# Re-opening four PSUM banks as single-bank tiles once attention has left them

## The chip, the cores and the metric

One core of a Trainium2 chip runs the whole program in one launch. The metric is the device time of the execution in microseconds (us). All runs told of here count as fast (within 1.5% of the fastest run of their kernel); where their clocks differ, in experiment 9, the text says so. The time of a run is some 1.8 us longer than the span of its profile. The granted TensorE clock of a profiled run is given where it matters. PE is the matmul engine (TensorE), PEld its weight loads, DVE is VectorE, ACT is ScalarE.

## The reference

Block-causal attention (8 batches, 8 heads, 576 positions, 64 per head) followed by a token mixer and a channel mixer over the model's 512 columns. The part that matters here is the channel mixer of the last batches, which runs after the last attention scores:

```python
u = x + (np.maximum(x.transpose(0, 2, 1) @ w_tok1, 0.0) @ w_tok2).transpose(0, 2, 1)
h2 = np.maximum(u @ w_ch1, 0.0) @ w_ch2     # w_ch1: 512 x 1536, w_ch2: 1536 x 512
out = u + h2
```

The kernel computes these products in seven block products instead of eight, which makes many evictions from PSUM: a block product is copied out (`keep`), added to another (`join`), or clipped at zero. The sums run on DVE, the copies and clips on DVE or ACT.

## The kernel before

The kernel holds eight banks of PSUM. Attention needs pairs of banks, because one exponential reads two banks at once (95 of them read 128x1024 from `sc` in the trace before, 1.02 us each by the median); everything else needs one. So the kernel has four single banks (`mm`) and two tiles of two banks (`sc`). When the last attention scores have been read, the four banks of `sc` go to a pool of slots named `late`, and matmuls take a slot from `mm` or from `late`.

```python
sc = ring(2, [128, 2, 512], FP32, "sc", psum)     # two tiles of two banks
mm = ring(4, [128, 512], FP32, "mm", psum)        # four tiles of one bank
...
P.pool("mm", mm)
P.pool("late", [])                                # empty until attention ends
BANK = ("mm", "late")
...
def bank_of(note):
    n = note["slot"]
    return mm[n] if note["pool"] == "mm" else sc[n // 2][:, n % 2]
...
# the exponentials of the last score set hand their two banks over as two slots each
freed = [[{"pool": "late", "slot": 2 * f + i} for i in range(2)] if last else None for f in range(2)]
...
# a block product takes a slot; its last reader gives it back
op = P.add("PE", mm_cost(512, 2), emit, deps + [last.get(to)], ..., take=[(BANK, bank)] if first else ())
...
with tc.manual_schedule():
    for op in P.search(1000):      # the order on each engine comes from a search at build time
        op.emit(op)
```

Two things do not see each other here. The search counts slots, so for it the two halves of an `sc` tile are independent. The layer that inserts the semaphores guards a tile: in the built program, a matmul into one half waits for the reader of the other half, and a reader of one half waits for matmuls into the other. The trace before shows both: the matmul at 205.82 us stood idle for 0.28 us by the profile's count, until the DVE add that read the other half had ended at 205.77 us, and the DVE copy at 261.57 us stood idle for 1.05 us while twelve matmuls went into the other half.

The softmax here doesn't subtract the row's maximum and nothing guards it: scores larger than these inputs give would overflow.

## Time and profile before

| | before |
|---|---|
| time, median of 3 (296.56 to 296.77) | 296.73 us |
| span of the profiled run | 294.8 us |
| PE busy in 196 to 232, 232 to 256, 256 to 272 us | 35.13, 23.95, 15.00 us |
| PE waits from 196 us on | four, all on `sc` banks, 1.7 us counted |

The way to read these: PE is busy almost all the time (285.8 us, 97% of the span), so only an idle gap of PE can be won. What such a gap really costs is worked out in the prediction below, which also shows the lines.

### The profile page before, as it was taken

How to read it: one execution, taken by the hardware profiler on the slowest of the kernel's cores; microseconds unless marked ns; L12 is line 12 of the kernel's file. 1: busy time of each engine (PE TensorE's matmuls, PEld its weight loads, DVE VectorE, ACT ScalarE, POOL GpSimd, SP SyncE). 2: the span in 40 equal slices, each digit the busy share in tenths (PEclk: the TensorE clock that was granted, in tenths of full speed). 3: DMA queues.
4: the chain of work that ended last, by engine and by line, in shares of the span. 5: the costliest groups of instructions: out<-in, count | busy, mean ns of one | idle time of the engine just before them, and what ended most of it. 6: DMA issues, size and time to landing. Idle time of an engine off the chain costs nothing.

```text
span 294.8 us, 7653 instructions
## 1 busy us (share of the span) xinstructions
PE 285.8 (97%) x3232; PEld 180.4 (61%) x3252; DVE 236.4 (80%) x512; ACT 166.9 (57%) x236; POOL 62.1 (21%) x96
## 2 busy tenths in 40 slices
PE   8999999999999999999999999999999999989994
PEld 4566456564557755545765567774446885556884
DVE  5566668988859979959988978678998968959993
ACT  5897874667776564786566685524476004847000
POOL 8776353810520260260050000000000000000000
PEclk9999999999999999999999999999999999999999
DMA  8999999993793399992359030041000811130054
GB/s 212 187 191 210 206 186 183 226 205 83 122 124 57 49 174 220 146 124 44 72 38 190 2 71 2 2 162 36 3 0 20 142 73 71 36 142 2 1 176 148
DMA packets 64403, 31.99 MB, mean 109 GB/s; under 512 B 53104, under 2 KB 55024, under 8 KB 64368
## 3 DMA queue, kind: packets, MB, share of 16 engines
q0 software_dynamic: 44320, 17.34, 50.1%
q1 hardware_dynamic: 19760, 13.57, 17.1%
q10 hardware_dynamic: 288, 0.59, 0.6%
q8 instruction: 25, 0.41, 0.5%
q14 instruction: 10, 0.08, 0.1%
HBM read 35.85 MB, written 9.44 MB: 154 GB/s over the span
## 4 chain that ended last, share of the span: by engine, by line
PE 87%; ACT 6%; DVE 4%; DMA 1%; issue 1%; ACTq 0%; DVEq 0%
PE mm L1221 17%; PE mm L992 15%; PE sc L548 9%; PE mm L595 9%; PE mm L1312 7%; PE mm L781 6%; PE sc L1097 5%; PE mm L1097 5%; PE sc L1221 4%; ACT e_sb L567 4%; PE mm L874 4%; PE mm L1019 3%; DVE turned L433 2%; DMA gT<-in_k_dram 1%; DVE gT L1125 1%
## 5 line engine op out<-in xcount | busy, mean ns | idle before, releaser
L567 ACT ACTIVATE e_sb<-sc 128x1024 bf16<-128x1024 f32 x95 | 92.5, 1030 | 32.9 <-PE sc L548 32.3
L992 PE MATMUL mm<-uT,wc_sb 128*128 128x512 bf16 x192 | 46.1, 382 | 0.0
L462 POOL DMA_DIRECT2D vals<-in_v_dram x45 | 37.0, 837 | 27.0 <-PE mm L595 22.4
L433 DVE STREAM_TRANSPOSE turned<-raws 128x288 int32<-128x288 int32 x64 | 40.2, 707 | 2.4 <-ACT raws L393 1.5
L548 PE MATMUL sc<-turned 32*128 32x64 bf16 (+4 forms) x744 | 35.4, 281 | 1.0 <-ACT e_sb L567 0.4
L595 PEld LDWEIGHTS <-e_sb 128*128 128x128 bf16 x896 | 31.3, 97 | 6.7 <-issue 3.2
L992 PEld LDWEIGHTS <-wc_sb 128*128 128x128 bf16 x192 | 20.0, 115 | 20.7 <-issue 5.7
L595 PE MATMUL mm<-vals,e_sb 128*128 128x65 bf16 x868 | 32.5, 193 | 0.1
L623 DVE TENSOR_TENSOR x_sb<-mm,rinv 128x320 bf16<-128x320 f32 x62 | 29.1, 485 | 1.3
L769 DVE TENSOR_SCALAR gT<-mm 128x512 bf16<-128x512 f32 x27 | 18.6, 688 | 10.9 <-PE mm L992 10.8
L1221 PEld LDWEIGHTS <-sums 128*128 128x128 bf16 x252 | 24.1, 98 | 4.5 <-issue 1.2
L1221 PEld LDWEIGHTS <-gT 128*128 128x128 bf16 x240 | 22.9, 98 | 4.5 <-issue 1.3
L548 PEld LDWEIGHTS <-turned 32*128 32x128 bf16 x752 | 12.8, 93 | 19.3 <-issue 16.7
L393 ACT COPY e_sb<-mm 128x512 f32<-128x512 f32 x14 | 8.2, 591 | 27.6 <-PE mm L1097 26.1
L767 ACT ACTIVATE gT<-mm 128x512 bf16<-128x512 f32 x24 | 14.3, 597 | 10.9 <-PE mm L992 10.8
L573 DVE MEMSET e_sb<- 64x128 uint32 (+1 forms) x72 | 10.6, 153 | 9.7 <-ACT e_sb L567 5.7
L781 PE MATMUL mm<-x_sb,w_sb 128*128 128x512 bf16 (+1 forms) x97 | 17.6, 313 | 0.3
L413 POOL DMA_DIRECT2D raws<-in_k_dram x15 | 8.2, 549 | 40.0 <-DVE turned L433 31.4
L889 DVE TENSOR_TENSOR u_sb<-mm,x_sb 128x512 bf16<-128x512 f32 x24 | 15.4, 684 | 1.4 <-PE sc L548 0.7
L1244 DVE TENSOR_TENSOR o_sb<-mm,u_sb 128x512 f32<-128x512 f32 x20 | 13.7, 687 | 3.4 <-PE mm L1221 2.6
L1097 PEld LDWEIGHTS <-raws 128*128 128x128 bf16 x96 | 9.2, 98 | 10.9 <-issue 1.5
L1221 PE MATMUL mm<-wd_sb,sums 128*128 128x256 bf16 x132 | 15.7, 273 | 0.0
(146 smaller groups left out, 458.0 us busy)
## 6 DMA issues: line engine op xcount, KB each, us to landing
out_dram<-o_sb SPq DMA_DIRECT2D x14, 512.0 KB, 3.2
raws<-in_k_dram POOLq DMA_DIRECT2D x15, 288.0 KB, 6.0
raws<-in_q_dram POOLq DMA_DIRECT2D x15, 288.0 KB, 6.8
vals<-in_v_dram POOLq DMA_DIRECT2D x28, 128.0 KB, 6.4
wc_sb<-in_moe_w_ch_dram POOLq DMA_DIRECT2D x8, 192.0 KB, 6.6
wc_sb<-in_moe_w_ch_dram POOLq DMA_DIRECT2D x3, 512.0 KB, 10.5
out_dram<-o_sb SPq DMA_DIRECT2D x10, 128.0 KB, 2.3
vals<-in_v_dram POOLq DMA_DIRECT2D x15, 64.0 KB, 5.6
```

The source lines that it names most:

```text
L433: nc.vector.transpose(dst[:, 0:S, :] .rearrange("p s e -> p (s e)") .bitcast(I32) .rearrange("p (a k) -> p k a", k=NB)[:, k0:k1], raw2.bit ...
L462: nc.gpsimd.dma_start(out=dst, in_=src)
L548: nc.tensor.matmul(out=home(n)[:, c0 : c0 + w], lhsT=kT[i][r, j0 : j0 + 128, par], rhs=qT[i][r, i0 : i0 + w, par], start=(par == 0), stop= ...
L567: nc.scalar.activation(dst, sc[SC.index(note["pool"])][:, :, 0:n], EXP, scale=scale)
L595: nc.tensor.matmul(out=u[:, I, 0:65], lhsT=w, rhs=vt[:, J, head, 0:65], start=(J == 0), stop=(J == I),)
L623: nc.vector.tensor_tensor(out=xt[:, :, 64 * head : 64 * head + 64], in0=u[:, :, 0:64], in1=ri.to_broadcast([128, 5, 64]), op=MULT,)
L769: nc.vector.tensor_scalar_max(dst, src, 0.0)
L781: nc.tensor.matmul(out=bank_of(bank)[:, w * n : w * n + w], lhsT=wt[:, tt : tt + 255 : 2], rhs=xt[:, c, cols], start=(c == 0), stop=(c == 4),)
L992: nc.tensor.matmul(out=bank_of(bank), lhsT=wc1_sb[:, m, channels(cc)], rhs=uT[b % 2][:, :, m, :], start=(m == 0), stop=(m == NDM - 1),)
L1097: nc.tensor.matmul(out=bank_of(bank), lhsT=x(m), rhs=y[:, :, m, :], start=first and m == 0, stop=m == 1, skip_group_check=not first,)
L1221: nc.tensor.matmul(out=bank_of(bank)[:, 256 * i : 256 * i + 256], lhsT=x[:, kk, 128 * i : 128 * i + 128], rhs=y[:, kk], start=first and i ...
L1312: nc.tensor.matmul(out=ps, lhsT=gt[:, cc, c0 : c0 + 128], rhs=wc2_sb[:, cc, cols], start=(cc == 0 and not turned), stop=(cc == NDC - 1),)
```

## The change

The intent is that the matmuls after attention see four single banks. The pool with the pairs is closed and a new pool is opened over the same memory at the moment when the first `late` slot is used. So that the pool of the pairs can be closed while that of `mm` stays open, `mm` is now allocated before `sc`.

```diff
-    sc = ring(2, [128, 2, 512], FP32, "sc", psum)
     mm = ring(4, [128, 512], FP32, "mm", psum)
+    held_banks = [tc.tile_pool(name="pairs", bufs=1, space=bass.MemoryType.PSUM)]
+    sc = ring(2, [128, 2, 512], FP32, "sc", held_banks[0].__enter__())
+    late = []
...
     def bank_of(note):
-        n = note["slot"]
-        return mm[n] if note["pool"] == "mm" else sc[n // 2][:, n % 2]
+        if note["pool"] == "mm":
+            return mm[note["slot"]]
+        if not late:
+            held_banks[0].__exit__(None, None, None)
+            held_banks[0] = tc.tile_pool(name="singles", bufs=1, space=bass.MemoryType.PSUM)
+            late.extend(ring(4, [128, 512], FP32, "late", held_banks[0].__enter__()))
+        return late[note["slot"]]
...
+    held_banks[0].__exit__(None, None, None)
```

## The prediction

> **What bounds the kernel now.** I read the page first, then busy time by stretch, then the waits of the matmul engine, then its timeline around each wait. The page's first section already says who is the bound:
>
> ```profile
> PE 285.8 (97%) x3232; PEld 180.4 (61%) x3252; DVE 236.4 (80%) x512; ACT 166.9 (57%) x236; POOL 62.1 (21%) x96
> ```
>
> The clock row of the page is 9 in all 40 slices, so no throttling is to be won back. The diff touches only tiles that are used after the last attention scores, and the timeline has the first matmul that writes one of those re-used banks (the weighted sum of values, L595 into `sc`) at 196.25 us. So I cut the span there; columns are stretch, its length, then busy us of PE, PEld, DVE, ACT, POOL:
>
> ```profile
> 0.00:196.00 196.00, 192.73 (x2532) 117.86 (x2549) 153.98 (x372) 131.41 (x178) 62.06 (x96) 1.00 0.91 129
> 196.00:232.00 36.00, 35.13 (x253) 19.95 (x254) 32.77 (x58) 16.35 (x29) 0.00 (x0) 1.00 0.18 39
> 232.00:256.00 24.00, 23.95 (x166) 16.40 (x165) 20.51 (x32) 7.69 (x13) 0.00 (x0) 1.00 0.30 80
> 256.00:272.00 16.00, 15.00 (x117) 9.63 (x117) 11.65 (x20) 10.97 (x17) 0.00 (x0) 1.00 0.18 67
> ```
>
> The change cannot act on the first 196 us. In the rest PE is idle for only 0.87, 0.05 and 1.00 us in the three stretches shown. Whatever is won is won out of those few gaps. The waits of PE from 196 us on name them all:
>
> ```profile
> PE sc L1097 <- DVE o_sb L1244: 0.9, 1, 0.9
> PE sc L1097 <- ACT e_sb L393: 0.5, 2, 0.3
> PE sc L874 <- DVE gT L1125: 0.3, 1, 0.3
> ```
>
> All four waits are for an `sc` bank, none for an `mm` bank: the single-bank tiles never hold PE up for long here, the paired ones do. The timeline shows what stood before each (start, length, engine, line, count, idle time):
>
> ```profile
> 204.94 0.59 PE L874 MATMUL mm<-aT,w_sb 128*128 128x512 bf16 x2
> 205.82 1.02 PE L874 MATMUL sc<-aT,w_sb 128*128 128x512 bf16 x4 [0.28 <-DVE gT L1125]
> ...
> 208.63 0.59 PE L1097 MATMUL mm<-e_sb,raws 128*128 128x512 bf16 x2
> 209.51 0.59 PE L1097 MATMUL sc<-uT,wc_sb 128*128 128x512 bf16 x2 [0.29 <-ACT e_sb L393]
> ...
> 219.59 0.59 PE L1097 MATMUL sc<-uT,wc_sb 128*128 128x512 bf16 x2
> 220.38 0.59 PE L1097 MATMUL sc<-e_sb,wc_sb 128*128 128x512 bf16 x2 [0.19 <-ACT e_sb L393]
> ...
> 261.37 0.59 PE L1097 MATMUL mm<-e_sb,wc_sb 128*128 128x512 bf16 x2
> 262.91 0.59 PE L1097 MATMUL sc<-uT,raws 128*128 128x512 bf16 x2 [0.95 <-DVE o_sb L1244]
> ```
>
> Pairs of matmuls that follow without a wait start 0.43 us apart (209.51 to 209.94 in the same timeline), so 0.216 us per matmul of 512 columns, though each row is longer. The idle time in brackets is counted from the modelled end; the time lost is counted from the start that the cadence would have given. That is more: 205.82 - (204.94 + 0.43) = **0.45**; 209.51 - 209.06 = **0.45**; 220.38 - 220.02 = **0.36**; 262.91 - 261.80 = **1.11** us.
>
> [...] here rows of 0.376 us start 0.216 us apart, which is why I reckon with starts.
>
> **The change part by part.** Its code is bookkeeping at build time. The schedule is chosen over slots, not tiles, and the comparison of the two built programs confirms that every engine has the same instructions in the same order (6,505 on PE, 513 on DVE, 239 on ACT); neither a copy nor a memset is added. What differs is the semaphore waits. I resolved each wait of both programs to the instruction that satisfies it. About 17 matmuls, 7 ScalarE and 13 VectorE instructions differ, of which these matter:
>
> 1. *Re-opening the pool.* The first matmul into a new tile gains a wait for the last score matmul, on its own engine and past. The last ScalarE exponential ended at 193.88 us, before 196.25. Cost 0.
> 2. *Matmul at 205.82* (second bank of pair 1) waited for a VectorE add that read the first bank (205.07 to 205.77). Gone; nothing else holds it. Gain 0.45.
> 3. *Matmul at 209.51* waited for the ScalarE copy at 208.88 of the other bank. What remains is its own bank's reader, a VectorE add done at 207.14. Gain 0.45.
> 4. *Matmul at 220.38* waited for the ScalarE copy at 219.74 of the other bank. What remains is an add at 219.02 to 219.70, which in the present timing alone would give nearly everything, and which itself moves up (see 6). Gain 0.36.
> 5. *Two small ones.* The matmul at 222.22 lost 0.12 us to an add on its neighbour: gone. The one at 219.16 loses 0.15 us to a true wait on an `mm` bank, whose add moves up: probably gone.
> 6. *VectorE reads that waited for matmuls into the neighbour.* The adds at 207.44 (0.30 us idle) and at 216.62 (0.57 idle) waited for a write to the other half. VectorE is busy 32.77 of 36 us there, so these count: without them VectorE keeps up with the earlier PE.
> 7. *Matmul at 262.91.* It waited for the add at 262.18, which stood behind a copy:
>
> ```profile
> 261.57 0.69 DVE L395 COPY e_sb<-sc 128x512 f32<-128x512 f32 x1 [1.05 <-PE sc L1221]
> 262.18 0.68 DVE L1244 TENSOR_TENSOR o_sb<-sc,u_sb 128x512 f32<-128x512 f32 x1
> ```
>
> The copy sat idle for 1.05 us for twelve L1221 matmuls into the other bank, although its own bank was complete at about 260.2. In the changed kernel it starts when VectorE is free (the add before it ends at 260.52), ends near 261.2, and the matmul needs only that copy: it starts at its natural 261.80. Gain 1.11.
>
> Sum: 0.45 + 0.45 + 0.36 + 0.12 + 0.15 + 1.11 = **2.64 us**. Nothing of it lies beside other work, because PE has no other idle time between 196 us and its last matmul.
>
> Will the earlier PE run into true waits? I took the slack between each matmul and the end of its other releasers, and moved both up. After 209 us PE is 0.9 us early and VectorE only about 0.45, then 0.57. Three matmuls become tight: those at 211.24, 214.26 and 216.42 come out at -0.02 to +0.07 us of slack. From 216.62 on VectorE is 1.2 us early and PE 0.9, then about 1.5 from 222 us. From 226 to 260 us slacks are 0.34 us or more and VectorE mostly follows PE. After 262.91 everything is 2.64 us early; the last stage has slacks of 0.4 or more that shift with PE. I allow 0.25 us for the tight places, so a gain of 2.4: 296.73 - 2.4 = **294.3 us**.
>
> **Rivals.** (a) *VectorE becomes the bound between 205 and 222 us and returns the early part.* For: it is 91% busy there, with almost no idle time from 210 to 216. Against: two of its own waits go too. It would leave the 1.11 us and perhaps half of the 1.5: about 295.0. (b) *The 262.91 wait is only moved*: the copy or the sums arrive as late for another reason. For: ScalarE's clip at 260.55 runs 1.06 us beside it. Against: it isn't a releaser of this matmul. It would cost most of 1.11: about 295.5. (c) *Nothing at all*, if waits through a semaphore's running count still cover the neighbour[...]. I counted in these; it would stay at 296.7. (d) *Slower*: a second drain of banks at the re-opening stalls PE. The resolved waits speak against it: no engine gains a late one.
>
> **Range and chances.** The measured runs differ by 0.2 us. A full gain with all tight places free gives 294.0, rivals (a) and (b) together 296. I take 293.7 to 295.4. A gain of over 2% would need 5.9 us, and PE has only 1.9 us of counted idle time in the three stretches: 1%. Slower by 2% needs a fault that neither program shows: 1%.
>
> **What would show it.** PE idle waits on re-used banks after 196 us should all but vanish (from 1.7 us in the list of waits to under 0.4). The copy of L395 before the old 262.91 place should no longer wait for L1221. The span up to 196 us should be the same to 0.1 us. New waits on `mm` banks, released by VectorE, near 210 to 216 us would be rival (a). The prediction is wrong if PE's idle time goes but the end doesn't move by it, or if earlier matmuls bring a slower cadence than 0.216 us.

## The result, and the profile after

The changed kernel took 294.19 us (median of 6, 294.04 to 294.74); the kernel before took 296.69 us in its 6 runs. The ratio is 0.9915 (95% interval 0.9902 to 0.9928). Ratios here are the mean time of one kernel's fast runs over that of the other's fast runs of the same rounds, so they are not quite the ratio of the medians. The prediction was 294.3 us.

The busy time by stretch of the changed kernel, with the columns of the prediction's table:

```profile
0.00:196.00 196.00, 194.18 (x2548) 117.83 (x2549) 153.53 (x372) 131.50 (x178) 61.97 (x96) 1.00 0.91 129
196.00:232.00 36.00, 36.00 (x269) 21.27 (x268) 33.89 (x60) 16.28 (x29) 0.00 (x0) 1.00 0.22 45
232.00:256.00 24.00, 24.00 (x166) 16.32 (x164) 20.48 (x33) 9.09 (x14) 0.00 (x0) 1.00 0.25 71
256.00:272.00 16.00, 16.00 (x128) 10.49 (x126) 12.90 (x21) 9.89 (x16) 0.00 (x0) 1.00 0.18 67
```

PE has no idle time at all from 196 us on, and the list of its waits from there is empty. (The first line counts 1.45 us more PE time than before, though the work is the same: the trace before has 20 fewer matmul records, 16 of them in this stretch.) The timeline of PE around two of the old waits, start, length, engine, line, count:

```profile
205.05 0.59 PE L881 MATMUL mm<-aT,w_sb 128*128 128x512 bf16 x2
205.48 1.03 PE L881 MATMUL late<-aT,w_sb 128*128 128x512 bf16 x4
...
259.97 0.59 PE L1104 MATMUL mm<-e_sb,wc_sb 128*128 128x512 bf16 x2
260.40 0.59 PE L1104 MATMUL late<-uT,raws 128*128 128x512 bf16 x2
```

Both pairs now start 0.43 us apart, which is two matmuls at the cadence: before, 0.88 and 1.54 us. On DVE, the copy that held the second of them no longer waits for L1228 (L1221 of the kernel before), while the add after it does, for its own bank:

```profile
259.22 0.69 DVE L402 COPY e_sb<-late 128x512 f32<-128x512 f32 x1
260.17 0.69 DVE L1251 TENSOR_TENSOR o_sb<-late,u_sb 128x512 f32<-128x512 f32 x1 [0.26 <-PE late L1228]
```

Because both programs have the same instructions in the same order, each matmul of one trace can be laid on its twin in the other. The difference of their starts changes at six places. In the rest it is flat, apart from places where a matmul's record is missing from the trace before:

| matmul, by its start before | predicted step, us | measured step, us |
|---|---|---|
| 205.82 | 0.45 | 0.45 |
| 209.51 | 0.45 | 0.45 |
| 219.16 | 0.15 | 0.15 |
| 220.38 | 0.36 | 0.35 |
| 222.22 | 0.12 | 0.12 |
| 262.91 | 1.11 | 1.11 |
| sum | 2.64 | 2.62 |

The profiled run of the changed kernel had started its first scores 0.13 us later and was still 0.11 us behind at 205 us, so PE ended 2.51 us earlier, 288.49 against 291.00 us. From there to the end of the span it took 3.92 us in place of 3.77, so that the span is 2.37 us shorter (292.40 against 294.77); why the end took longer was not looked into. The medians differ by 2.50.

### The profile page after: what moved, and what is told of

It reads as the page before. It is cut to its first block, busy times and chain, and to the rows that moved or that the text cites. A ratio compares the mean times of both kernels' runs of the same rounds, so it can differ in the third digit from the quotient of the medians.

```text
span 292.4 us, 7674 instructions
## 1 busy us (share of the span) xinstructions
PE 286.7 (98%) x3252; PEld 180.4 (62%) x3252; DVE 235.7 (81%) x512; ACT 166.8 (57%) x236; POOL 62.0 (21%) x96
## 4 chain that ended last, share of the span: by engine, by line
PE 93%; ACT 4%; DVE 1%; issue 0%
PE mm L1228 18%; PE mm L999 15%; PE sc L555 9%; PE mm L602 9%; PE mm L1319 7%; PE mm L1104 6%; PE late L1104 6%; PE mm L788 6%; PE late L1228 4%; PE mm L881 4%; ACT e_sb L574 4%; PE mm L1026 3%; PE mm L372 2%; DVE turned L440 1%; PE mm L912 1%; PE mm L379 0%
## 5 line engine op out<-in xcount | busy, mean ns | idle before, releaser
L1228 PEld LDWEIGHTS <-sums 128*128 128x128 bf16 x252 | 24.1, 98 | 4.4 <-issue 1.2
L1228 PEld LDWEIGHTS <-gT 128*128 128x128 bf16 x240 | 22.9, 98 | 4.5 <-issue 1.3
L1251 DVE TENSOR_TENSOR o_sb<-mm,u_sb 128x512 f32<-128x512 f32 x20 | 13.7, 686 | 3.4 <-PE mm L1228 2.6
L1228 PE MATMUL mm<-wd_sb,sums 128*128 128x256 bf16 x132 | 15.7, 273 | 0.0
L1251 DVE TENSOR_TENSOR o_sb<-mm,o_sb 128x512 f32<-128x512 f32 (+1 forms) x19 | 12.0, 631 | 4.4 <-PE mm L1228 4.2
```

The source lines that it names most:

```text
L1228: nc.tensor.matmul(out=bank_of(bank)[:, 256 * i : 256 * i + 256], lhsT=x[:, kk, 128 * i : 128 * i + 128], rhs=y[:, kk], start=first and i ...
L1251: nc.vector.tensor_tensor(out=dst, in0=src, in1=other, op=ADD)
```

## The experiments

The theory is that the width of the guarded tile sets the price: matmuls and readers of different banks wait for one another when one tile covers both. A false wait is a wait for a reader or a matmul of another bank, which only the shared tile imposes. The rivals are that the re-opening or the new order of the pools did it, that each false wait is worth just what its own matmul lost (the local account, against the chain theory, by which a wait can pass its delay on through DVE and ACT), and that the last stage was short of banks. Twelve runs were made, two of them repeats; all gave correct results, and that narrower guards are safe is shown by no more than this. Each ratio is to the kernel before. The edits below are to the changed kernel unless said otherwise.

**1. Re-opened as two pairs.**

```diff
-            late.extend(ring(4, [128, 512], FP32, "late", held_banks[0].__enter__()))
-        return late[note["slot"]]
+            late.extend(ring(2, [128, 2, 512], FP32, "late", held_banks[0].__enter__()))
+        return late[note["slot"] // 2][:, note["slot"] % 2]
```

> As the changed kernel, with the banks re-opened as two tiles of two banks, slots 0+1 and 2+3 as before. My theory (the width of the tile that is guarded is all that counts): every false wait is back, at the old places (matmuls near 205.8, 209.5, 220.4 and 262.9 us), 296.7 us, within 0.3 of the kernel before. Rival (the closing and re-opening of the pool, or the other order of the PSUM pools, is what gained): 294.2 us.

Measured: 296.86 us, ratio to before 1.000 (0.9992 to 1.0008). The four waits were back at 205.83, 209.49, 220.34 and 262.88 us. So neither the closing and re-opening nor the order of the pools gains or costs anything that can be seen (the interval is 0.24 us either way): the gain is in the width of the tile.

**2 and 3. Only one of the pairs split.** In the first, slots 0 and 1 are single and 2 and 3 are one tile; in the second, the other way round.

```diff
-            late.extend(ring(4, [128, 512], FP32, "late", held_banks[0].__enter__()))
+            again = held_banks[0].__enter__()
+            singles = ring(2, [128, 512], FP32, "late", again)
+            pair = ring(1, [128, 2, 512], FP32, "latepair", again)[0]
+            late.extend(singles + [pair[:, 0], pair[:, 1]])    # second kernel: pair first, then singles
```

> Only slots 0 and 1 become single banks; 2 and 3 stay one tile. Local account (each matmul's own false wait is worth what it lost): 0.12 + 1.11 = 1.2 us gained, 295.45 us. Theory of chains: VectorE's add near 216.6 us, which waited for a neighbour in pair 0, also starts some 0.6 us earlier; the ScalarE copy behind the wait near 220.4 us (a pair 2+3 wait that stays in this kernel) then ends in time, and so does the true wait near 219.2 us. Gained 0.15 + 0.36 + 0.12 + 1.11 = 1.75 us, so 294.95 us, with the false waits at 205.8 and 209.5 still there (0.45 us each) and none near 220.

> Only slots 2 and 3 become single banks; 0 and 1 stay one tile. Local account: 0.45 + 0.45 + 0.36 = 1.26 us gained, 295.4 us. Theory of chains: the two early gains of 0.45 stay, but VectorE still loses time to false waits in pair 0, so what is won near 220.4 us is lost again at the wait near 222.2 us, which grows from 0.12 to about 0.46 us; gained 0.9 us, 295.8 us. The 1.1 us wait near 262.9 us (then near 262.0) is still there in either case.

Measured: with slots 0 and 1 split, 295.38 us, ratio 0.9948 (0.9935 to 0.9961), which lay between the two accounts; with slots 2 and 3 split, 295.90 us, ratio 0.9969 (0.9956 to 0.9982), that is 0.9 us gained (0.5 to 1.3), where the chain theory had 0.9 and the local account 1.26. This interval takes in both, so the traces have to tell. Their PE waits after 196 us follow, all of them (the edits move the lines: L1097 of the kernel before is L1107 and L1106 here). First with slots 0 and 1 split:

```profile
206.45 0.59 PE L884 MATMUL latepair<-aT,w_sb 128*128 128x512 bf16 x2 [0.28 <-DVE gT L1135]
210.10 0.59 PE L1107 MATMUL latepair<-uT,wc_sb 128*128 128x512 bf16 x2 [0.24 <-ACT e_sb L403]
```

Then those with slots 2 and 3 split:

```profile
221.47 0.59 PE L1106 MATMUL latepair<-e_sb,raws 128*128 128x512 bf16 x2 [0.31 <-DVE gT L1134]
262.15 0.59 PE L1106 MATMUL latepair<-uT,raws 128*128 128x512 bf16 x2 [0.95 <-DVE o_sb L1253]
```

The first trace has no wait near 220 us, although the tile of slots 2 and 3 is still a pair there: the 0.36 us that the matmul at 220.38 lost before was the price of pair 0, handed on by DVE and ACT. In the repeat told of below, with no late start, the DVE add at 216.62 starts at 215.96, and the ACT copy that held this matmul starts at 219.23 in place of 219.74. The second trace shows the reverse. It won 0.36 us at 220.38, and the matmul that stood at 222.22 before lost 0.47 us by its start in place of 0.12; in all its PE gained 0.87 us from 205 us on. The profiled run of the first kernel had begun its scores 0.6 us late, long before the change can act; laid on the trace before, its matmuls gained 1.77 us from 205 us on. As the time was not as clear as the trace, it was run again beside the changed kernel:

> The changed kernel unchanged, run beside the next two on one chip for a comparison: 294.2 us, 2.5 us under the kernel before (2.3 to 2.7), no wait of PE on a re-used bank after 196 us.

> Slots 0 and 1 single once more, because the first time lay between the two theories (1.54 us gained; chains 1.75, local account 1.24) and its profiled run began 0.6 us late, before the change can act. Chains: 0.85 us over the changed kernel of the same rounds (the two waits of 0.45 us that stay), so 295.05 us. Local account: 1.26 us over it, 295.45 us.

Measured: the changed kernel 294.15 us, ratio 0.9907 (0.9893 to 0.9920); slots 0 and 1 split 295.04 us, ratio 0.9938 (0.9924 to 0.9952). The difference of the medians is 0.89 us, against 0.85 of the chain theory and 1.26 of the local account. The traces say the same: laid on the trace before, PE gained 1.77 us in the split kernel and 2.62 in the changed one. The chain theory holds, the local account falls: what removing only some of the false waits wins adds up only if the chain is followed.

**4 and 5. The same two-bank tiles, other neighbours.** Slots 0+2 and 1+3, then 0+3 and 1+2.

```diff
+            late.extend(ring(2, [128, 2, 512], FP32, "late", held_banks[0].__enter__()))
-        return late[note["slot"]]
+        return late[note["slot"] % 2][:, note["slot"] // 2]                 # 0+2, 1+3
+        return late[(0, 1, 1, 0)[note["slot"]]][:, note["slot"] // 2]       # 0+3, 1+2
```

> Two tiles of two banks again, but slots 0+2 and 1+3 are neighbours. If the price is set by which groups of matmuls happen to share a tile, the old four waits go and others come: from the waits of this program laid over the measured durations I estimate 0.78, 0.25, 0.75, 0.73 us between 207 and 218 us, about 1.7 us between 247 and 258 us, and 0.5 us after; 4.8 us more than the changed kernel, so 299.0 us (298.3 to 299.7). If two-bank tiles cost the same whoever shares them: 296.7 us.

> The third way to pair the four slots: 0+3 and 1+2. Same theory as for 0+2: by the waits of this program over the measured durations, 1.15, 0.29, 0.71, 0.24, 0.34, 0.99 us between 207 and 224 us and about 1.1 us in small waits later, 4.9 us more than the changed kernel: 299.1 us (298.3 to 299.8). The wait near 262.9 us should be gone. Rival (pairs all cost alike): 296.7 us.

Measured: 299.28 us, ratio 1.0081 (1.0067 to 1.0096), and 299.39 us, ratio 1.0089 (1.0072 to 1.0106). Both are within 0.3 us of what the waits of their programs gave, and 2.4 to 2.5 us slower than the old pairing re-opened in experiment 1. The old pairing was the cheapest of the three. So the width alone does not set the price; which slots share a tile does too.

**6. One tile of four banks.**

```diff
+            late.extend(ring(1, [128, 4, 512], FP32, "late", held_banks[0].__enter__()))
-        return late[note["slot"]]
+        return late[0][:, note["slot"]]
```

> All four re-opened banks are one tile of four banks. If the width of the guard sets the price, a wider one must cost more than any pairing: my estimate from the waits of this program over the measured durations is some 20 waits on PE, 13.7 us more than the changed kernel, about 308 us (304 to 311). Rival (the price does not follow the width): about 297 us.

Measured: 309.12 us, ratio 1.0412 (1.0397 to 1.0428), 15 us over the changed kernel where some 13.7 were expected. In 196 to 232 us PE was busy for 29.06 us, where the changed kernel has 36.00. The longest waits of its timeline:

```profile
209.63 0.59 PE L1104 MATMUL late<-e_sb,raws 128*128 128x512 bf16 x2 [1.00 <-DVE um_sb L929]
...
225.54 0.59 PE L1104 MATMUL late<-uT,wc_sb 128*128 128x512 bf16 x2 [0.97 <-ACT e_sb L400]
229.52 0.59 PE L1104 MATMUL late<-e_sb,raws 128*128 128x512 bf16 x2 [1.66 <-ACT e_sb L400]
```

So with the same order and the same banks the time goes 294.2, 296.9, 309.1 us as the guard goes from one to two to four banks.

**7. The other four banks made pairs.**

```diff
-    mm = ring(4, [128, 512], FP32, "mm", psum)
+    mm = [t[:, i] for t in ring(2, [128, 2, 512], FP32, "mm", psum) for i in range(2)]
```

> The changed kernel, with the other four banks (mm, used all through) made two tiles of two banks: the same false sharing put where it was never present. If it is a general mechanism, PE, busy over 98% of the span now, gets many new waits on mm banks: an estimate of 10 us in the last 100 us, and with the 190 us before it 20 to 40 us in all, so 315 to 335 us. Rival (only the mixture of stages after attention is sensitive): 305 us or less, with no new waits before 190 us.

Measured: 329.99 us, ratio 1.1124 (1.1099 to 1.1150). The list of PE waits (us in total, times, longest) has some 30 new entries, on products of every stage; the largest are:

```profile
PE mm L1228 <- DVE o_sb L1251: 2.9, 4, 1.2
PE mm L999 <- DVE u_sb L896: 2.6, 2, 1.7
PE mm L881 <- DVE u_sb L896: 2.1, 4, 0.6
```

PE was busy for 91.07 and 88.63 us of the first two hundreds, where the changed kernel has 98.18 and 100.00, so the waits lie in the attention stages too. The mechanism isn't special to the last stage.

**8. Half the banks, no re-opening.** This is an edit to the kernel before: the second bank of each pair isn't used after attention.

```diff
-            freed = [[{"pool": "late", "slot": 2 * f + i} for i in range(2)] if last else None for f in range(2)]
+            freed = [[{"pool": "late", "slot": 2 * f}] if last else None for f in range(2)]
```

> Another way out of the false waits, on the kernel before: the second bank of each left pair is not used at all, so six single banks serve the last 100 us in place of eight, nothing is re-opened, and the schedule is searched anew for six banks. If the false waits alone cost the 2.5 us and two banks fewer cost nothing, 294.2 us. If the last stage needs eight banks (slacks between a matmul and the end of its bank's last reader were 0.3 to 1 us in the kernel before), the matmuls wait for true readers instead: my guess is 297 to 302 us, 299 in the middle, with waits of PE on mm and sc banks spread over 205 to 275 us.

Measured: 295.81 us, ratio 0.9966 (0.9953 to 0.9978), so the guess of 299 was wrong. With six banks PE had no wait after 196 us. The losses that the trace shows came at the start, in an order that the search had found anew: five waits on score banks, 1.8 us in total, four of them, 1.6 us, before 21 us. The busy time of 8 to 20 us (the number after POOL is the granted PE clock), first of this kernel:

```profile
8.00:20.00 12.00, 10.47 (x147) 6.62 (x145) 5.11 (x21) 9.32 (x17) 9.13 (x17) 0.72 1.51 186
```

and of the changed kernel:

```profile
8.00:20.00 12.00, 11.67 (x187) 7.09 (x186) 6.86 (x27) 10.96 (x20) 9.14 (x16) 1.00 1.50 177
```

The clock is the second loss: it was 0.50 from 11.99 to 18.82 us and 1.00 just before and after. Matmuls of 256 columns start 0.21 us apart in that stretch, and 0.11 us apart in the changed kernel, at a granted clock of 1.00. Three counted PE waits, of 0.60, 0.28 and 0.46 us, ended at 9.98, 10.89 and 12.04 us, around the fall of the clock; whether they caused it was not tested. Six single banks are enough for the last stage, in the order found for them; it isn't the number of banks that was short. Whether the whole 1.7 us against the changed kernel is that early order, and how much of it the waits and how much the clock cost, was argued and not shown. The next pair was to tell.

**9 and 10. A longer search, with six banks and with the change.** The edit is `P.search(4000)` for `P.search(1000)`.

> The six-bank kernel with 4000 tries of the schedule search in place of 1000. The six-bank run had no PE wait after 196 us, and its loss against the changed kernel, 1.66 us, matches the waits that its newly searched order has between 9 and 29 us (1.7 us of idle time against 0.4). If that is accident of the search and six banks do suffice, another search may mend it: 294.2 us (293.9 to 295.8 by what order it finds) and again no wait after 196 us. If six banks are the limit, 295.8 us with waits on mm or sc banks in the last 100 us.

> The changed kernel with 4000 tries. PE is never idle after 196 us and only some 1.6 us before it, so a longer search has little to win: 294.1 us (293.6 to 294.8). If its early order comes out worse by chance, as in the six-bank run, up to 295.8 us.

Measured: with six banks 295.84 us, but its 14 runs spread from 295.26 to 299.28, four of them over 298; ratio 0.9990 (0.9964 to 1.0017). Those four had a mean clock of 0.975 to 0.977, the other ten 0.988 to 0.994. The profiled run again had no PE wait after 196 us, but 2.0 us of waits on score banks before 29 us, and the clock was again 0.50 for 6.83 us from 11.37 us on (0.88 on average over 0 to 29 us). So the longer search didn't mend its start, and the run is inconclusive on what six banks could reach. With the change, 293.15 us, ratio 0.9876 (0.9863 to 0.9889): it beats both kernels and lies below the 293.6 to 294.8 us that were expected. Its last matmul ended 0.4 us earlier than the changed kernel's (288.07 against 288.49 us), and from there to the end of the span it took 3.3 us in place of 3.9. The kernel before was not run with 4000 tries, so how much of this needs the change is open.

## Why the prediction was right

The predicted 294.3 us against 294.19 measured, and the parts hold one by one.

- *Re-opening costs nothing*: experiment 1, with the re-opening and without the split, is at a ratio of 1.000.
- *The four counted waits and the two small ones*: all are gone, and each step of the shift between the traces is within 0.01 us of its term. Reckoning by starts instead of the idle time in brackets was needed: the bracketed waits come to 1.7 us, and 2.5 were won.
- *VectorE's false waits count*: the prediction said so and gave no price. Experiments 2 and 3 give one. Where pair 0 stays, what is won at 220.38 is lost again at 222.22 (0.47 us); where pair 0 alone is split, the wait at 220.38 is gone although its own pair remains. So item 4 had its size right and its cause only in part: it named the guard of its own pair, but splitting that pair alone only moved the 0.36 us to the next wait.
- *The 0.25 us allowed for tight places* was not used. The matmuls at 211.24, 214.26 and 216.42 lost nothing; the shift is flat from 209.5 to 219 us. It is the one term that was mis-sized, 0.25 for 0. The profiled run of the repeat, which did not start late, has the whole 2.62 us at PE's end and 2.53 at the end of the span. That the predicted gain of 2.4 us comes so near to the 2.50 between the medians is thus partly luck: an allowance that was not needed stood in for a small loss after the last matmul (0.14 and 0.09 us in the two profiled runs) that the prediction did not have.
- *Rivals*: DVE as the new bound (a) did not appear: no new wait of PE, and DVE went from 32.77 to 33.89 us of 36. The wait at 262.91 (b) was not moved. Waits covered by other semaphores (c) would have left the time at 296.7. A stall at the re-opening (d) is in no trace.

## What to carry to other kernels

When PSUM is carved into tiles of several banks, look at what the waits guard: here a matmul that waited for a reader of another bank showed as a short wait on just that tile (four of 0.19 to 0.95 us, all on `sc`), and making the tile one bank wide removed it without touching an instruction. Price such waits by the starts of the matmuls and by the chain behind them, because a wait seen at one tile can be the debt of another (the 0.36 us at 220.38 was that of pair 0). The order may be worth searching again afterwards: 4000 tries gave the changed kernel a further 1.0 us. Whether the kernel before would have won as much was not run.
